# Chaining block products in pairs in PSUM, prelu on ScalarE and VectorE one step apart, and the next splits issued ahead of PSUM copies

## The chip, the cores and the metric

One core of one Trainium2 chip runs the whole program. The metric is the device time of one execution in microseconds (us); the median of three runs before the change is 1681.34 us (1676.72 to 1686.11).

## What is computed

Three stages follow one another. An attention with 32 packed queries per head feeds a first mixture block (product, rational function, product), and its result feeds a second block. The change touches the second block and the passage into it:

```
def _moe2_ref(x, w_in, w_out, alpha):        # x 4608 x 512, w_in 512 x 2048, w_out 2048 x 512
    h = x @ w_in
    g = np.maximum(h, 0.0) + alpha * np.minimum(h, 0.0)     # prelu
    return (g @ w_out).astype(np.float32)
```

## The kernel before

Every product is made of three passes in the fp32r type (`PASSES`): an operand is split into a rounded part (a copy on ScalarE) and the remainder (a subtraction on VectorE or GpSimd). The two parts are needed before a matmul can read the operand.

The second block works on five superblocks of tokens (`SUPER`, index s from 0): four with 2 x 512 tokens and a last one with 2 x 256. A superblock has two halves. The first half (y = 0, called L3 in the code, matmuls in L1018) makes h, the second half (y = 1, L4, matmuls in L1029) makes the output. Each half uses a seven-product block scheme (Strassen and Winograd): products i = 0 to 6, each cut into four pieces n = 0 to 3. A piece is a *unit* of 12 matmuls; a half has 28 units, whose place from 0 to 27 is called the *position* here. `UNITS` holds the order.

In the first half each unit fills a PSUM tile `p` of two banks (pool `psn`, four tiles in turn). When a unit is done, `end_L3` takes it out: a copy or a relu on ScalarE, or an add on VectorE onto a block `v` of h (`add`, L855). Products 0 and 1 share a tile already: the first is copied out, then the second is accumulated onto it in the same banks. Blocks that are complete go through the prelu: `prelu_dve` (two relus on ScalarE, two fused multiply-adds on VectorE, L873) or, for the pieces of products 4 and 3, `prelu_pool` (relu, two scaled copies and relu on ScalarE, L865, L879, L880, then an add on GpSimd, L881). `split_v` splits a block of h for the second half (L947 on ScalarE, L948 on VectorE); `split_y` does it for the input (L781, L782).

All engines execute in program order. The loop over units sets that order: at step u it issues the matmuls of unit u, then `after()` (the taking out of unit u-1), then the tasks that `at(u, ...)` has put there (splits and sums), and in the first superblock `w_split(u + 5)`, which splits a weight tile (L750 ScalarE, L751 GpSimd in the first half and VectorE in the second) that `w_load` had brought. Later superblocks read the split weights back from DRAM by `w_load(u + 12)`.

Before that, the loop over g ends the first mixture block. In its last three rounds (g >= NG, d = 0, 1, 2) it loads and splits the first eight weight tiles through three staging tiles (`s2_tile`).

## Time and profile before

| | |
|---|---|
| profiled execution | 1680.22 us (span of its core 1678.3 us) |
| median of three runs | 1681.34 us |
| second block, first to last matmul | 867.86 to 1674.45 us of the span |
| granted TensorE clock, mean | 0.968 |

Times within the profile are microseconds from the start of the span. PE is TensorE's matmuls, PEld its weight loads, DVE VectorE, ACT ScalarE, POOL GpSimd. The granted clock is a share of full speed. In a timeline, equal neighbours are merged (x7), and a bracket tells how long the engine was idle before the row and what it had waited for. In a table of stretches a row holds the stretch, its length, the busy time and count of PE, PEld, DVE, ACT and POOL, the granted clock, the busy share of the DMA engines and the GB/s that they moved.

### The profile page before, as it was taken

How to read it: one execution, taken by the hardware profiler on the slowest of the kernel's cores; microseconds unless marked ns; L12 is line 12 of the kernel's file. 1: busy time of each engine (PE TensorE's matmuls, PEld its weight loads, DVE VectorE, ACT ScalarE, POOL GpSimd, SP SyncE). 2: the span in 40 equal slices, each digit the busy share in tenths (PEclk: the TensorE clock that was granted, in tenths of full speed). 3: DMA queues.
4: the chain of work that ended last, by engine and by line, in shares of the span. 5: the costliest groups of instructions: out<-in, count | busy, mean ns of one | idle time of the engine just before them, and what ended most of it. 6: DMA issues, size and time to landing. Idle time of an engine off the chain costs nothing.

```text
span 1678.3 us, 20312 instructions
## 1 busy us (share of the span) xinstructions
PE 1534.8 (91%) x7360; PEld 1237.5 (74%) x7360; DVE 1326.0 (79%) x1424; ACT 1036.5 (62%) x1209; POOL 658.0 (39%) x386
## 2 busy tenths in 40 slices
PE   5789869999999999999989779996999799979988
PEld 3444447888888888888868657885888588857878
DVE  5979699899999999999976479665856485648657
ACT  2335377878888888877855765446443744364353
POOL 1113165778788887866665600022001200130020
PEclk9999989999999999999999979998999899989999
DMA  9688822133333333321348447974475447444784
GB/s 346 229 286 280 285 90 76 57 113 120 112 103 114 109 129 99 128 75 51 113 156 294 171 165 273 400 309 148 163 272 182 173 176 253 157 181 158 274 319 139
DMA packets 134404, 305.44 MB, mean 182 GB/s; under 512 B 11680, under 2 KB 63904, under 8 KB 133280
## 3 DMA queue, kind: packets, MB, share of 16 engines
q1 hardware_dynamic: 130848, 291.56, 49.9%
q10 hardware_dynamic: 3456, 12.58, 2.0%
q8 instruction: 59, 0.97, 0.2%
q14 instruction: 41, 0.34, 0.1%
HBM read 221.79 MB, written 82.31 MB: 181 GB/s over the span
## 4 chain that ended last, share of the span: by engine, by line
PE 53%; DVE 23%; ACT 13%; issue 6%; DMA 3%; POOL 1%; SPq 0%; ACTq 0%; DVEq 0%; POOLq 0%
PE p L1029 15%; PE acc L622 13%; PE p L1018 12%; PE h L548 9%; ACT r L865 3%; DVE v L855 3%; DVE vsp L948 2%; ACT r L879 2%; ACT v L880 2%; DVE h L606 2%; DVE s L670 2%; PE pp L329 1%; DVE s L662 1%; ACT vsp L947 1%; DVE s L663 1%
## 5 line engine op out<-in xcount | busy, mean ns | idle before, releaser
L1029 PE MATMUL p<-vsp,ws 128*128 128x512 f32 (+1 forms) x1680 | 379.8, 387 | 59.3 <-issue 25.1
L622 PE MATMUL acc<-gt,wo 128*128 128x512 f32 x1728 | 406.9, 391 | 3.6 <-ACT yo L564 3.6
L1029 PEld LDWEIGHTS p<-vsp,ws 128*128 128x128 f32 x1680 | 307.7, 199 | 131.4 <-issue 31.0
L622 PEld LDWEIGHTS acc<-gt,wo 128*128 128x128 f32 x1728 | 322.1, 188 | 70.3 <-ACT yo L564 4.6
L1018 PE MATMUL p<-ysp,ws 128*128 128x512 f32 (+1 forms) x1680 | 351.5, 371 | 16.6 <-DVE v L855 6.8
L1018 PEld LDWEIGHTS p<-ysp,ws 128*128 128x128 f32 x1680 | 294.6, 190 | 73.0 <-ACT v L887 7.2
L881 POOL TENSOR_TENSOR v<-v,r 128x1024 f32<-128x1024 f32 (+1 forms) x40 | 87.0, 2175 | 610.5 <-ACT v L880 606.5
L548 PE MATMUL h<-a2t,wb 128*128 128x128 f32 (+7 forms) x1536 | 250.7, 319 | 20.1 <-DVE v__1751 L607 5.4
L548 PEld LDWEIGHTS h<-a2t,wb 128*128 128x128 f32 x1536 | 229.3, 192 | 42.5 <-issue 20.0
L948 DVE TENSOR_TENSOR vsp<-v,vsp 128x1024 fp32r<-128x1024 f32 (+1 forms) x140 | 160.5, 1156 | 75.6 <-ACT vsp L947 75.3
L947 ACT ACTIVATE vsp<-v 128x1024 fp32r<-128x1024 f32 (+1 forms) x140 | 132.5, 966 | 108.9 <-PE p L1029 55.3
L855 DVE TENSOR_TENSOR v<-v,p 128x1024 f32<-128x1024 f32 (+1 forms) x120 | 129.8, 1108 | 42.8 <-PE p L1018 42.6
L865 ACT ACTIVATE r<-v 128x1024 f32<-128x1024 f32 (+1 forms) x60 | 58.0, 966 | 162.5 <-DVE v L855 162.5
L873 DVE SCALAR_TENSOR_TENSOR v<-r,nalpha,v 128x512 f32<-128x512 f32 (+1 forms) x80 | 56.4, 747 | 71.6 <-ACT v L870 71.6
L855 DVE TENSOR_TENSOR v<-v 128x1024 f32<-128x1024 f32 (+1 forms) x80 | 88.6, 1113 | 0.0
L502 POOL TENSOR_TENSOR wb<-s,wb 128x512 fp32r<-128x512 f32 x48 | 63.1, 1315 | 31.1 <-ACT wb L501 30.6
L358 POOL TENSOR_TENSOR trn<-trn,mx 128x576 f32<-128x576 f32 x16 | 20.1, 1255 | 111.0 <-DVE mx L357 101.8
L670 DVE SCALAR_TENSOR_TENSOR s<-s,s 128x512 int32<-128x512 int32 x40 | 62.4, 1560 | 0.3
L662 DVE TENSOR_SCALAR s<-s 128x512 f32<-128x512 f32 x40 | 57.5, 1437 | 0.0
L782 DVE TENSOR_TENSOR ysp<-yq,ysp 128x1024 fp32r<-128x1024 f32 (+1 forms) x28 | 37.0, 1325 | 24.6 <-ACT ysp L781 24.6
L409 PE MATMUL pw<-w_in,pph 128*128 128x512 f32 x96 | 50.3, 637 | 4.0 <-ACT wbs L421 3.9
L879 ACT ACTIVATE r<-r,nalpha 128x512 f32<-128x512 f32 (+1 forms) x80 | 50.1, 673 | 1.3
(1032 smaller groups left out, 2353.5 us busy)
## 6 DMA issues: line engine op xcount, KB each, us to landing
ws<-wh_d SPq DMA_DIRECT2D x224, 512.0 KB, 6.1
wh_d<-ws SPq DMA_DIRECT2D x56, 512.0 KB, 4.3
wq_d<-s SPq DMA_DIRECT2D x32, 512.0 KB, 3.8
wb_d<-wbs SPq DMA_DIRECT2D x48, 256.0 KB, 4.9
s<-in_w_out SPq DMA_DIRECT2D x24, 512.0 KB, 4.2
s<-wb_d SPq DMA_DIRECT2D x48, 256.0 KB, 4.0
wst<-wq_d SPq DMA_DIRECT2D x48, 256.0 KB, 3.2
kt<-in_kT SPq DMA_DIRECT2D x16, 576.0 KB, 7.8
```

What stands on the lines that cost most here:

```text
L548: mm(h[:, ft, o:o + m], w[x][:, k, 128 * ft:128 * ft + 128], a2_t[c][:, y, k, o:o + m], start=n == 0, stop=n == 5)
L622: mm(acc[d // 2][:, d % 2, :], w[:, x, 128 * d:128 * d + 128], t[:, y, ft, :], start=f == 0 and (x, y, ft) == (0, 0, 0), stop=f == NP - 1 ...
L662: dve.tensor_scalar(w, w, LOW, HIGH, op0=ALU.max, op1=ALU.min)
L670: dve.scalar_tensor_tensor(wi, in0=words[:, :, 0], scalar=29, in1=wi, op0=ALU.logical_shift_right, op1=ALU.bitwise_or)
L855: dve.tensor_tensor(o, a, b, op=op)
L865: act(r, src, AF.Relu, scale=-1.0)
L879: act(r[:, g], r[:, g], AF.Copy, scale=nalpha[:, f:f + 1])
L881: pool.tensor_tensor(v_, v_, r, op=ALU.add)
L947: act(t[:, 0, :, 0:m], src, AF.Copy)
L948: dve.tensor_tensor(t[:, 1, :, 0:m], src, t[:, 0, :, 0:m], op=ALU.subtract)
L1018: mm(ps[:, g, 0:m], w[:, g, x, 128 * k:128 * k + 128], ysp[s, i](z, k), start=i != 1 and q == 0, stop=q == 5, skip_group_check=i < 2)
L1029: mm(ps[:, d, 0:m], w[:, g, x, 128 * d:128 * d + 128], t[:, z, g, 0:m], start=i != 1 and n == 0 and g == 0 and q == 0, stop=n == 3 and g = ...
```

## The change

1. Two more pairs of products share a PSUM tile in the first half: 3 is accumulated onto 6, and 2 onto 4, in the interleaved order that 0 and 1 had (`ONTO`, `PAIRED`). The blocks of h take the sums as they stand in PSUM, so `end_L3` has one add where product 4 had two, and a sign of the input sums changes.
2. Every prelu is now two relus on ScalarE and two fused multiply-adds on VectorE. `prelu` issues the relus and returns the rest, which the loop issues one step later (`defer`). GpSimd adds and scaled copies are gone.
3. At step u the loop first issues the ScalarE copies of splits (`early`), then `after()`, then the rest of the unit before (`last()`), then sums (`late`), then the subtractions of the splits (`rests`).
4. The splits of the first four units of the second half move from positions 24 to 27 of the first half to 14, 19, 21 and 26. The input's splits and loads move forward, too.
5. The first eight weight tiles are loaded from round d = -1 on, each into a place of its own, and their remainders are made on VectorE. The negation of alpha moves to the same place.

```diff
-    FIRST = ((0, 0), (0, 1), (1, 0), (0, 2), (1, 1), (0, 3), (1, 2), (1, 3))
-    UNITS = [[*FIRST, *((i, n) for i in (5, 6, 4, 3, 2) for n in range(4))],
+    PAIRED = [(x, n) for x, n in ((0, 0), (0, 1), (1, 0), (0, 2), (1, 1), (0, 3), (1, 2), (1, 3))]
+    UNITS = [[((0, 1)[x], n) for x, n in PAIRED] + [(5, n) for n in range(4)] + [((6, 3)[x], n) for x, n in PAIRED]
+             + [((4, 2)[x], n) for x, n in PAIRED],
              [(i, n) for i in (0, 2, 1, 5, 4, 6, 3) for n in range(4)]]
+    ONTO = ({1: 0, 3: 6, 2: 4}, {1: 0})
...
         act(t[:, :, 0], st, AF.Copy)
-        eng.tensor_tensor(t[:, :, 1], st, t[:, :, 0], op=ALU.subtract)
+        return lambda: eng.tensor_tensor(t[:, :, 1], st, t[:, :, 0], op=ALU.subtract)
...
-        if g >= NG:
-            d = g - NG
+        d = g - NG
+        if d == -1:
+            pool.tensor_scalar(nalpha, alpha_sb, -1.0, None, op0=ALU.mult)
+            for n, st in enumerate((gp.tile([128, 2, CH], F32, tag="ast", name="wst", bufs=1),
+                                    spa.tile([128, 2, CH], F32, tag="q_", name="wst", bufs=2))):
+                for x in range(2):
+                    w_load(2 * n + x, st[:, x])
+        elif d >= 0:
             if d == 0:
-                for u in range(3):
-                    w_load(u)
-            else:
-                split_y(0, d - 1, y_block(0, d - 1, 0))
-            for u in range(3 * d, min(3 * d + 3, SOON)):
-                w_split(u, pool)
-                if u + 3 < SOON:
-                    w_load(u + 3)
+                for n, tag in ((2, "v_"), (3, "q_")):
+                    st = spa.tile([128, 2, CH], F32, tag=tag, name="wst", bufs=2)
+                    for x in range(2):
+                        w_load(2 * n + x, st[:, x])
+            for u in range(4 * d, min(4 * d + 4, SOON)):
+                w_split(u, dve)()
+            if d:
+                split_y(0, d - 1, y_block(0, d - 1, 0))()
...
-    def prelu_dve(v_, src, a, n, m):
-        r = neg_part(src, m)
-        act(v_, src, AF.Relu)
...
-    def prelu_pool(v_, a, n, m):
-        r = neg_part(v_, m)
-        for g in range(2):
-            f = HF * a + 2 * n + g
-            act(r[:, g], r[:, g], AF.Copy, scale=nalpha[:, f:f + 1])
-        act(v_, v_, AF.Relu)
-        pool.tensor_tensor(v_, v_, r, op=ALU.add)
+    def prelu(v_, src, a, n, m):
+
+        r = cols(half_tile("r", "r", 3), m)
+        act(r, src, AF.Relu, scale=-1.0)
         act(v_, src, AF.Relu)
...
+        def rest():
+            for g in range(2):
+                f = HF * a + 2 * n + g
+                dve.scalar_tensor_tensor(v_[:, g], in0=r[:, g], scalar=nalpha[:, f:f + 1], in1=v_[:, g], op0=ALU.mult, op1=ALU.add)
+        return rest
...
         elif i == 6:
-            add(v_tile(1, 0, n, m), v12, p)
+            add(v_tile(1, 1, n, m), u2, p)
+        elif i == 3:
+            add(v_tile(1, 0, n, m), u2, p)
+            return prelu(V[1, 0, n], V[1, 0, n], 1, n, m)
         elif i == 4:
-            add(v_tile(1, 1, n, m), V[1, 0, n], p)
-            add(v12, v12, p)
-            prelu_pool(V[1, 1, n], 1, n, m)
-        elif i == 3:
-            add(V[1, 0, n], V[1, 0, n], p, ALU.subtract)
-            prelu_pool(V[1, 0, n], 1, n, m)
+            add(V[1, 1, n], V[1, 1, n], p)
+            return prelu(V[1, 1, n], V[1, 1, n], 1, n, m)
         else:
-            add(v12, v12, p)
-            prelu_dve(v12, v12, 0, n, m)
+            add(u2, u2, p)
+            return prelu(u2, u2, 0, n, m)
...
-        for d, step in ((0, 0), (1, 1), (2, 2), (3, 3), (6, 10), (9, 8), (14, 7), (18, 6)):
-            at(u0 + d, y_sums, s, step)
+        for d in range(4):
+            then(u0 + (0, 0, 1, 3)[d], y_sum, s, d)
+        for d, i in ((3, 5), (6, 6), (7, 3), (9, 4), (10, 2)):
+            at(u0 + d, y_part, s, i)
         if s + 1 < len(SUPER):
-            at(u0 + 20, load_y, s + 1)
+            then(u0 + 13, load_y, s + 1)
         u1 = u0 + NU2
         for d in range(NU2):
-            at(u1 + d - 4, split_v, u1 + d)
+            at(u1 + (d - 4 if d >= 4 else (-14, -9, -7, -2)[d]), split_v, u1 + d)
...
-        if after:
-            after()
+        rests = [f(*args) for f, args in early.pop(u, ())]
+        if u < len(units) and s == 0 and SOON <= u + 5 < 2 * NU2:
+            rests.append(w_split(u + 5, dve if units[u + 5][1] else pool))
+        last, defer = defer, after and after()
+        if last:
+            last()
+        for f, args in late.pop(u, ()):
+            f(*args)
+        for f in rests:
+            f()
+        after = None
```

On PE, in the first half of the first superblock, positions 12 to 19: a row is one unit, p_... its PSUM tile. Before:

```order
L1018 MATMUL p_7456<-ysp_7335,ws_7362 128x512 x12
L1018 MATMUL p_7476<-ysp_7335,ws_7387 128x512 x12
L1018 MATMUL p_7497<-ysp_7335,ws_7410 128x512 x12
L1018 MATMUL p_7521<-ysp_7335,ws_7430 128x512 x12
L1018 MATMUL p_7542<-ysp_7407,ws_7450 128x512 x12
L1018 MATMUL p_7563<-ysp_7407,ws_7470 128x512 x12
L1018 MATMUL p_7591<-ysp_7407,ws_7491 128x512 x12
L1018 MATMUL p_7622<-ysp_7407,ws_7515 128x512 x12
```

and with the change:

```order
L1025 MATMUL p_7458<-ysp_7327,ws_7354 128x512 x12
L1025 MATMUL p_7478<-ysp_7327,ws_7378 128x512 x12
L1025 MATMUL p_7458<-ysp_7352,ws_7405 128x512 x12
L1025 MATMUL p_7525<-ysp_7327,ws_7430 128x512 x12
L1025 MATMUL p_7478<-ysp_7352,ws_7451 128x512 x12
L1025 MATMUL p_7571<-ysp_7327,ws_7471 128x512 x12
L1025 MATMUL p_7525<-ysp_7352,ws_7491 128x512 x12
L1025 MATMUL p_7571<-ysp_7352,ws_7516 128x512 x12
```

Eight tiles filled once each have become four filled twice, with one or two other units between the two fillings.

On VectorE, end of the first half of the second superblock (v<-v,p is the add out of PSUM, the fused rows the prelu, vsp the remainder of a split). Before, steps 14 to 26:

```order
L782 TENSOR_TENSOR ysp<-yq,ysp 128x1024
L855 TENSOR_TENSOR v<-v,p 128x1024 x6
L782 TENSOR_TENSOR ysp<-yq,ysp 128x1024
L855 TENSOR_TENSOR v<-v,p 128x1024 x8
L948 TENSOR_TENSOR vsp<-v,vsp 128x1024
L855 TENSOR_TENSOR v<-v,p 128x1024
L873 SCALAR_TENSOR_TENSOR v<-r,nalpha,v 128x512 x2
L948 TENSOR_TENSOR vsp<-v,vsp 128x1024
```

and with the change, step 21 to the start of step 26:

```order
L868 TENSOR_TENSOR v<-v,p 128x1024
L885 SCALAR_TENSOR_TENSOR v<-r,nalpha,v 128x512 x2
L954 TENSOR_TENSOR vsp<-v,vsp 128x1024
L868 TENSOR_TENSOR v<-v,p 128x1024
L885 SCALAR_TENSOR_TENSOR v<-r,nalpha,v 128x512 x2
L868 TENSOR_TENSOR v<-v,p 128x1024
L885 SCALAR_TENSOR_TENSOR v<-r,nalpha,v 128x512 x2
L868 TENSOR_TENSOR v<-v,p 128x1024
L885 SCALAR_TENSOR_TENSOR v<-r,nalpha,v 128x512 x2
L868 TENSOR_TENSOR v<-v,p 128x1024
L885 SCALAR_TENSOR_TENSOR v<-r,nalpha,v 128x512 x2
L868 TENSOR_TENSOR v<-v,p 128x1024
```

Fourteen adds stood around an input split, and only then came the first split for the second half and the last adds with their prelus; now every add is followed by the prelu of the unit before it, and splits for the second half stand among them.

On ScalarE at the same end (vsp is the rounded part of a split). Before:

```order
L879 ACTIVATE r<-r,nalpha 128x512 x2
L880 ACTIVATE v<-v 128x1024
L865 ACTIVATE r<-v 128x1024
L879 ACTIVATE r<-r,nalpha 128x512 x2
L880 ACTIVATE v<-v 128x1024
L947 ACTIVATE vsp<-v 128x1024
L865 ACTIVATE r<-v 128x1024
L870 ACTIVATE v<-v 128x1024
L947 ACTIVATE vsp<-v 128x1024
L865 ACTIVATE r<-v 128x1024
```

and with the change:

```order
L880 ACTIVATE v<-v 128x1024
L879 ACTIVATE r<-v 128x1024
L880 ACTIVATE v<-v 128x1024
L953 ACTIVATE vsp<-v 128x1024
L879 ACTIVATE r<-v 128x1024
L880 ACTIVATE v<-v 128x1024
L879 ACTIVATE r<-v 128x1024
L880 ACTIVATE v<-v 128x1024
L953 ACTIVATE vsp<-v 128x1024
L879 ACTIVATE r<-v 128x1024
L880 ACTIVATE v<-v 128x1024
L953 ACTIVATE vsp<-v 128x1024 x4
```

The first split for the second half stood behind all eight prelus of products 4 and 3; now the fourth and the fifth split stand among the last prelus, three more stand further ahead, and the later ones follow without a prelu between.

## Rows read from the trace of the kernel before

**Rows 1.** The page, busy time (us), share of the span and instructions of each engine.

```profile
PE 1534.8 (91%) x7360; PEld 1237.5 (74%) x7360; DVE 1326.0 (79%) x1424; ACT 1036.5 (62%) x1209; POOL 658.0 (39%) x386
```

**Rows 2.** Ten half superblocks: us, PE PEld DVE ACT POOL busy (x), clock, DMA, GB/s.

```profile
867.86:967.79 99.93, 81.06 (x338) 64.98 (x336) 57.12 (x44) 60.93 (x81) 59.24 (x35) 0.92 0.68 237
967.79:1062.93 95.14, 86.73 (x337) 67.46 (x337) 81.92 (x87) 53.81 (x66) 0.00 (x0) 0.92 0.70 247
1062.93:1146.52 83.59, 76.60 (x338) 62.83 (x336) 45.91 (x40) 43.67 (x51) 19.18 (x8) 0.98 0.84 332
1146.52:1234.52 88.00, 81.54 (x337) 65.06 (x338) 66.71 (x61) 40.51 (x40) 0.00 (x0) 0.96 0.48 168
1234.52:1318.11 83.59, 76.58 (x338) 62.83 (x336) 45.91 (x40) 43.69 (x51) 19.17 (x8) 0.98 0.63 227
1318.11:1406.12 88.01, 82.52 (x337) 65.95 (x338) 66.71 (x61) 40.52 (x40) 0.00 (x0) 0.95 0.47 167
1406.12:1489.70 83.58, 76.58 (x337) 62.82 (x336) 45.91 (x40) 43.67 (x51) 19.19 (x8) 0.99 0.61 214
1489.70:1578.91 89.21, 83.30 (x337) 66.54 (x337) 65.64 (x61) 39.88 (x40) 0.00 (x0) 0.93 0.46 165
1578.91:1625.60 46.69, 40.70 (x338) 40.35 (x336) 25.90 (x40) 25.70 (x51) 10.30 (x8) 0.99 0.93 361
1625.60:1674.45 48.85, 45.06 (x336) 43.26 (x336) 35.01 (x59) 22.21 (x38) 0.00 (x0) 0.94 0.43 146
```

**Rows 3.** Timeline of PE alone: start, us, instructions merged, idle before and releaser.

```profile
1062.93 60.00 PE L1018 MATMUL p<-ysp,ws 128*128 128x512 f32 x264
1123.26 16.60 PE L1018 MATMUL p<-ysp,ws 128*128 128x512 f32 x72 [0.33 <-PE p L1018]
...
1318.11 8.58 PE L1029 MATMUL p<-vsp,ws 128*128 128x512 f32 x24 [6.67 <-issue]
...
1578.91 31.83 PE L1018 MATMUL p<-ysp,ws 128*128 128x256 f32 x264
...
1655.60 18.85 PE L1029 MATMUL p<-vsp,ws 128*128 128x256 f32 x155 [0.34 <-DVE vsp L948]
```

**Rows 4.** Timeline of all engines, third superblock, end of first half, start of second.

```profile
1289.90 2.59 DVE L782 TENSOR_TENSOR ysp<-yq,ysp 128x1024 fp32r<-128x1024 f32 x1 [3.87 <-ACT ysp L781]
1292.41 7.99 DVE L855 TENSOR_TENSOR v<-v,p 128x1024 f32<-128x1024 f32 x7
...
1300.38 2.41 POOL L881 TENSOR_TENSOR v<-v,r 128x1024 f32<-128x1024 f32 x1 [0.85 <-ACT v L880]
1300.60 1.22 DVE L855 TENSOR_TENSOR v<-v,p 128x1024 f32<-128x1024 f32 x1 [0.19 <-PE p L1018]
...
1313.28 1.04 ACT L947 ACTIVATE vsp<-v 128x1024 fp32r<-128x1024 f32 x1
1313.45 2.34 POOL L881 TENSOR_TENSOR v<-v,r 128x1024 f32<-128x1024 f32 x1 [0.89 <-ACT v L880]
1314.35 2.52 DVE L948 TENSOR_TENSOR vsp<-v,vsp 128x1024 fp32r<-128x1024 f32 x1 [12.53 <-ACT vsp L947]
1316.80 1.21 DVE L855 TENSOR_TENSOR v<-v,p 128x1024 f32<-128x1024 f32 x1
...
1320.28 1.42 DVE L873 SCALAR_TENSOR_TENSOR v<-r,nalpha,v 128x512 f32<-128x512 f32 x2 [2.27 <-ACT v L870]
1321.61 1.22 DVE L948 TENSOR_TENSOR vsp<-v,vsp 128x1024 fp32r<-128x1024 f32 x1
```

**Rows 5.** Timeline of all engines at the start of the first superblock.

```profile
872.00 1.99 ACT L750 ACTIVATE ws<-s 128x512 fp32r<-128x512 f32 x3 [7.60 <-DMA s<-wq_d]
...
880.21 6.10 PE L1018 MATMUL p<-ysp,ws 128*128 128x512 f32 x18 [6.75 <-ACT v L887]
```

**Rows 6.** Timeline of all engines, second half of the first superblock.

```profile
1007.49 0.69 DVE L751 TENSOR_TENSOR ws<-wst,ws 128x512 fp32r<-128x512 f32 x1
```

More of the change, by code (lines that the diff above doesn't have):

```diff
@@ L1018, in attention_then_two_moes @@
                             mm(ps[:, g, 0:m], w[:, g, x, 128 * k:128 * k + 128], ysp[s, i](z, k),
[L1019 removed]
+                               start=not onto and q == 0, stop=q == 5, skip_group_check=again)
                             q += 1
             else:
[L1022 to L1024 removed]
                 t = vsp.pop(u)
@@ L1036, in attention_then_two_moes @@
                 after = lambda a=(s, i, n, ps): end_L3(*a)
-            else:
-                after = (lambda a=(s, i, ps): end_L4(*a)) if n == 3 else None
-            for f, args in tasks.pop(u, ()):
-                f(*args)
-            if s == 0 and u + 5 < 2 * NU2 and u + 5 >= SOON:
-                w_split(u + 5, dve if units[u + 5][1] else pool)
-    assert not tasks
+            elif n == 3:
+                after = lambda a=(s, i, ps): end_L4(*a)
+    assert not early and not late and not defer
     for name in ("spb", "spy", "psn"):
```

100 lines of the change are left out of this document (47 added, 53 removed).

## Prediction

> **What bounds the kernel now.** I read the page's busy times first [rows 1]. PE is busy for 91% of the span and DVE for 79%: PE is the engine to follow, and the question is where its other 9% and its slow stretches lie. Outside the second block the change moves only the last rounds ahead of it, so I cut that block at the starts of its ten halves [rows 2]. The reader is to see there that a first half of a full superblock takes 83.6 us (99.9 in the first superblock) and a second half 88.0 to 95.1, although both issue 336 matmuls of one shape, and that the granted clock is 0.92 to 0.99 in them.
>
> What would a half take without a stop? PE's own timeline [rows 3] shows 264 matmuls in 60.00 us, with no idle time inside: 0.2273 us each, so 336 x 0.2273 = 76.4 us a half and 12 x 0.2273 = 2.73 us a unit. For the last superblock it shows 264 in 31.83 (0.1206 each, 40.5 us) and 155 in 18.85 (0.1216, 40.9 us), 1.45 us a unit. Taken from the lengths in [rows 2]:
>
> - first superblock: 99.93 - 76.4 = 23.5 and 95.14 - 76.4 = 18.7
> - second: 7.2 and 11.6; third: 7.2 and 11.6; fourth: 7.2 and 12.8
> - last: 46.69 - 40.5 = 6.2 and 48.85 - 40.9 = 8.0
>
> Together 114.0 us. This is all that the change can bring, as it takes no matmul away: 1680.2 - 114.0 = 1566.2 us is the floor.
>
> Next, what makes the stops. Around the end of a first half all engines together [rows 4] show one chain. DVE stands 3.87 us for an input split whose rounded part ScalarE had not made, needs 2.59 us for it, and then does seven adds out of PSUM in 7.99 us that had piled up. Behind them ScalarE still has the prelus of products 4 and 3, so the first split for the second half starts on it at 1313.28, its remainder is done at 1316.87, and the next add, which empties the PSUM tile that the second half wants first, ends at 1318.01. PE had stopped 6.67 us before 1318.11 [rows 3]. Then every unit waits for one round of add, relu, relu, fused multiply-adds and split, which shows as DVE's 2.27 us waits. The first 24 matmuls after the stop take 8.58 us where 24 x 0.2273 = 5.46 are needed: they run partly at the lower of the two clock levels (1.2 GHz, against 2.4). In the first superblock ScalarE stands 7.60 us for a weight tile's DMA, the first copy out of PSUM queues behind it, and PE idles 6.75 us [rows 5].
>
> **The change part by part, on DVE.** A row of seven adds in 7.99 us gives 1.14 us for each in a full queue. The two fused multiply-adds and the next instruction start 1321.61 - 1320.28 = 1.33 us apart [rows 4]. I take 1.14 for a split's remainder too.
>
> *Chaining.* Product 4 loses its second add: 4 x 1.14 = 4.6 us of DVE per superblock, which is off the path where DVE keeps up. The new condition: PE may start on a tile again only when the add of the first product has read it. At the tightest places (products 6 and 3, pieces 0 and 3; 4 and 2 likewise) one unit of 2.73 us lies between. The add is first in DVE's step, starts about 0.2 us after the unit's end (idle 0.19 in [rows 4]) and lasts 1.22: 1.4 us, done with 1.3 us to spare, if DVE isn't late by more than that.
>
> *Is DVE late?* From step 20 to 27 each step has one add and one prelu: 1.14 + 1.33 = 2.47 of 2.73 us. The splits at steps 21 and 26 add 1.14 each, so DVE falls 0.9 us behind, regains 0.26 a step, and is 1.1 behind at the end. Steps 28 and 29, with the last prelus, first sums and splits, bring 4.75 and 3.61 us: 3.1, then 4.0 behind, after which a step has 2.28 and it recovers. The split for position 32 is made at step 28: done about 1.1 + 4.75 = 5.9 us after that step's start, where 4 x 2.73 = 10.9 are allowed. The four units before it have splits from steps 14 to 26. So PE should pass from half to half without a stop in the second, third and fourth superblock. In the sum over a half: DVE's 45.9 us [rows 2] plus 12 prelus at 1.33 and three splits at 1.14 make 65.3 of 76.4 us.
>
> *Prelu off GpSimd.* 40 adds on POOL and 80 scaled copies on ScalarE go; ScalarE then has two relus and a split at most in a step. What POOL does besides: the split at 1314.35 takes 2.52 us while POOL runs, the one at 1321.61 takes 1.22 alone, and the add out of PSUM at 1300.60 takes 1.22 in the midst of a POOL add [rows 4]. An instruction of DVE with both inputs in SBUF pays 1.30 us beside POOL. That ends in the later superblocks. In the first one `w_split` stays on POOL up to step 22, and prelus now stand on DVE there. Steps 12 to 22 hold 11 adds, 5 prelus and 3 splits: 22.6 us of 30.0. If all eight instruction groups from SBUF met POOL, 8 x 1.30 = 10.4 us would come on top, 3.0 too many; if half did, nothing. I take 1.5, between 0 and 3.0.
>
> The Trainium skill speaks on this in "SBUF — State Buffer", Who interferes with whom: an instruction of VectorE with two SBUF inputs and one of GpSimd that reads SBUF exclude each other for the whole instruction. The two splits agree with it; by that rule alone, with every group meeting POOL, the term would be the 3.0 and the sum 1583.2.
>
> *First superblock, border and second half.* From step 23 a weight remainder comes to each DVE step (0.69 us [rows 6], 0.6 in a full queue): 3.07 us a step against 2.73, so DVE is 1.7 us behind at step 26 where one unit separates the fillings of the last tile, a stop of 0.3 to 2.6 us. I take 2.0. In the second half sums, splits and remainders make 2.9 us a step for eleven steps; behind by 7 to 8 us, it uses up the 10.9 allowed near position 39. I take 1.0, from 0 to 4.
>
> *Entry.* All eight weight tiles get places of their own and are loaded before the last rounds, so the 7.60 us wait goes. New: their remainders are eight instructions on DVE beside POOL's last work, 8 x 0.6 = 4.8 us, ahead of the input's split. Between 0 and 5 us late; I take 2.5.
>
> *Later superblocks.* The three borders: 0 to 6 each (the old stop is 6.67), I take 1.0 by the step count above, together 3.0. The last superblock has units of 1.45 us; with half the elements an add and a prelu cost somewhat over half, about the unit itself: 0 to 4, I take 1.5. Its weight loads are covered: with PE never waiting in its first half DMA moved 361 GB/s at a share of 0.93 [rows 2]. Small waits like the 0.33 us in [rows 3]: 0.4 a half, 4.0.
>
> **Sum.** What stays: 2.5 + 1.5 + 2.0 + 1.0 + 3.0 + 1.5 + 4.0 = 15.5 us. Gain 114.0 - 15.5 = 98.5, time 1680.2 - 98.5 = 1581.7, say **1582 us**. The profiled execution lies 1.1 us under the median of 1681.34, too little to correct for. All low ends give 1570.5 with the small waits, 1566.5 without; all high ends (5, 3.0, 2.6, 4, 18, 4, 4.0: 40.6) give 1606.8.
>
> **Rivals.**
>
> *DVE becomes the bound.* If a step costs single durations (1.22 + 1.42 = 2.64) and one hand-over like the 0.19 us idle, it is 2.83 of 2.73 us at steps 20 to 27, and with the splits DVE never regains: about 8 x 0.1, two splits at 1.2 and 2.9 for steps 28 and 29, 6 us of stop a border, 30 us over five, and some 10 more in the first superblock's second half, where DVE is busy 81.92 of 95.14 already. 1582 + 40 = 1622, between 1607 and 1640. For: 65 of 76 us is full. Against: seven adds in 7.99 us show no gap where work is queued.
>
> *The chained tiles stop PE (slower).* 40 units (8 a superblock) newly wait for a tile to be read before they may start. If DVE's queue blocks as at 1289.90, 3.87 + 2.59 = 6.46 us before the add, each waits 6.46 - 2.73 = 3.7 us: 40 x 3.7 = 148 us, and 1582 + 148 = 1730. It decides from (1688.6 - 1581.7) / 40 = 2.7 us a unit on: there the time is 8.4 us over before. For: all forty adds stand in one queue with prelus that wait for ScalarE. Against: the prelu comes a step later, when its relus are done, and products 0 and 1 are chained already and show 264 matmuls without a stop [rows 3].
>
> The Trainium skill has a rule for that side in "TensorE: Matmul & The Clock Gate", A second HAM failure mode: psum-queue depth-cycling: a kernel that cycles through PSUM banks idles PE briefly between groups, and its clock goes up and down. The trace doesn't agree yet: the first halves cycle through four tiles, with stops only at the borders.
>
> *It doesn't do what it says.* The stops shift to another place, say splits that wait for their buffers (five for input and blocks together), and most of the 114 us stay: within 8 us of before.
>
> **How the numbers follow.** Forecast (1566 to 1607) 0.74; DVE bound 0.16; stops shifted 0.04; slower 0.06. A measurement of this kernel tells about 0.5%, 8.4 us, from no change. Faster 0.74 + 0.16 = 0.90, same 0.04, slower 0.06. The range goes from 1567, just over the floor, to 1616, which takes in the forecast's high ends and the nearer part of the DVE case: 0.74 + 0.06 = 0.80.
>
> **What would show it.** Right: halves of 76 to 79 us in the second to fourth superblock, a clock of 0.99 or 1.00 in all ten, no PE idle time over 1 us at the change of halves, DVE busy near 65 us in a first half, POOL at 0 after the first superblock. Wrong: PE waits in L1025 for DVE's add at position 14, 19, 22 or 27 (chained tiles), waits in L1033 for DVE's remainder (DVE bound), or a first superblock over 165 us in all (entry or weights).

## The result, and the profile after

The changed kernel takes 1566.31 us (median of four runs, 1563.95 to 1568.25) against 1682.2 us (median of four, 1676.72 to 1686.11: the three known ahead of the prediction and one more): a ratio of 0.9313, 95% interval 0.9283 to 0.9343. The forecast was 1582 us, 1567 to 1616. The sign and the main mechanism came out as forecast; the gain is larger, 115.9 us against 98.5, and the median lies 0.7 us under the range.

The profiled execution took 1565.32 us (span 1563.4). Its page begins with the busy times that answer to [rows 1]:

```profile
PE 1494.1 (96%) x7360; PEld 1221.8 (78%) x7360; DVE 1350.6 (86%) x1492; ACT 995.5 (64%) x1129; POOL 560.8 (36%) x338
```

Cut at the starts of the ten halves, as [rows 2] (columns: us; PE, PEld, DVE, ACT, POOL busy with instructions; clock; DMA share; GB/s):

```profile
862.57:945.28 82.71, 78.61 (x337) 63.79 (x336) 71.59 (x71) 54.47 (x67) 31.67 (x20) 0.98 0.81 285
945.28:1021.70 76.42, 76.42 (x337) 63.24 (x336) 72.87 (x78) 45.73 (x56) 0.00 (x0) 1.00 0.83 297
1021.70:1097.86 76.16, 76.16 (x337) 63.06 (x336) 56.85 (x60) 41.81 (x42) 0.00 (x0) 1.00 0.89 346
1097.86:1174.02 76.16, 76.16 (x338) 63.06 (x336) 59.47 (x54) 33.82 (x33) 0.00 (x0) 1.00 0.59 201
1174.02:1250.18 76.16, 76.16 (x338) 63.06 (x336) 56.85 (x60) 41.81 (x42) 0.00 (x0) 1.00 0.70 240
1250.18:1326.34 76.16, 76.16 (x338) 63.06 (x336) 59.47 (x54) 33.81 (x33) 0.00 (x0) 1.00 0.59 202
1326.34:1402.50 76.16, 76.16 (x338) 63.06 (x336) 56.85 (x60) 41.81 (x42) 0.00 (x0) 1.00 0.68 227
1402.50:1478.66 76.16, 76.16 (x338) 63.06 (x336) 58.41 (x54) 32.95 (x33) 0.00 (x0) 1.00 0.59 202
1478.66:1519.07 40.41, 40.41 (x338) 40.37 (x337) 31.98 (x59) 23.84 (x41) 0.00 (x0) 1.00 0.96 375
1519.07:1559.55 40.48, 40.47 (x338) 40.27 (x336) 31.86 (x53) 18.72 (x31) 0.00 (x0) 1.00 0.60 218
```

From 945.28 us to the end PE's busy time equals the length of every half to 0.01 us: no stop is left, at a clock of 1.00 where [rows 2] had 0.92 to 0.99. The second block takes 696.98 us, 109.6 fewer than the 806.59 of before, and it starts 5.3 us earlier (862.57 against 867.86).

What is left stands in the first superblock. PE's timeline there (start, us, merged instructions, idle before and its releaser):

```profile
862.57 0.61 PE L1025 MATMUL p<-ysp,ws 128*128 128x512 f32 x2
864.60 60.03 PE L1025 MATMUL p<-ysp,ws 128*128 128x512 f32 x262 [1.41 <-DVE ysp L788]
924.83 13.88 PE L1025 MATMUL p<-ysp,ws 128*128 128x512 f32 x60 [0.20 <-DVE v L868]
941.10 4.38 PE L1025 MATMUL p<-ysp,ws 128*128 128x512 f32 x12 [2.38 <-ACT vsp L953]
```

The 2.38 us stop is unit 27's. The profile names a split of ScalarE, whose record ends at 941.02 us; VectorE's own timeline shows the add that frees the tile, unit 25's, from 939.74 to 940.95. The run without the chain (below) decides between the two: there unit 27 has a tile of its own and ends at 945.00, without a stop, before the same split of ScalarE starts at 946.95. So unit 27 waited for the add:

```profile
936.68 1.21 DVE L868 TENSOR_TENSOR v<-v,p 128x1024 f32<-128x1024 f32 x1
...
939.14 0.68 DVE L753 TENSOR_TENSOR ws<-wst,ws 128x512 fp32r<-128x512 f32 x1
939.74 1.21 DVE L868 TENSOR_TENSOR v<-v,p 128x1024 f32<-128x1024 f32 x1
```

Add to add is 3.06 us: the step of 3.07 that the prediction counted with a weight remainder in it.

VectorE at the border of the second superblock, without those remainders:

```profile
1079.02 1.22 DVE L868 TENSOR_TENSOR v<-v,p 128x1024 f32<-128x1024 f32 x1 [0.17 <-PE p L1025]
1080.16 1.41 DVE L885 SCALAR_TENSOR_TENSOR v<-r,nalpha,v 128x512 f32<-128x512 f32 x2
1081.48 1.22 DVE L954 TENSOR_TENSOR vsp<-v,vsp 128x1024 fp32r<-128x1024 f32 x1
1082.62 1.22 DVE L868 TENSOR_TENSOR v<-v,p 128x1024 f32<-128x1024 f32 x1
...
1085.08 1.21 DVE L868 TENSOR_TENSOR v<-v,p 128x1024 f32<-128x1024 f32 x1
...
1087.53 1.21 DVE L868 TENSOR_TENSOR v<-v,p 128x1024 f32<-128x1024 f32 x1
...
1089.99 1.22 DVE L868 TENSOR_TENSOR v<-v,p 128x1024 f32<-128x1024 f32 x1
```

The add at 1079.02 starts 0.17 us after its unit's end, 1078.85. With 2.72 us a unit the next ends are 1081.57, 1084.29, 1087.01, 1089.73, and the adds start 1.05, 0.79, 0.52 and 0.26 us behind them: one split puts VectorE 0.9 us back, each step of 2.46 us regains 0.26. Both numbers stand in the prediction. By step 26, whose add is the one that unit 27 waits for, VectorE has caught up: that add starts at 1092.62, 0.2 us after its unit's end.

### The profile page after: what moved, and what is told of

It reads as the page before. It is cut to its first block, busy times and chain, and to the rows that moved or that the text cites. A ratio compares the mean times of both kernels' runs of the same rounds, so it can differ in the third digit from the quotient of the medians.

```text
span 1563.4 us, 20124 instructions
## 1 busy us (share of the span) xinstructions
PE 1494.1 (96%) x7360; PEld 1221.8 (78%) x7360; DVE 1350.6 (86%) x1492; ACT 995.5 (64%) x1129; POOL 560.8 (36%) x338
## 4 chain that ended last, share of the span: by engine, by line
PE 69%; DVE 20%; issue 4%; ACT 4%; DMA 3%; POOL 0%; SPq 0%; ACTq 0%; DVEq 0%; POOLq 0%
PE p L1033 22%; PE p L1025 20%; PE acc L621 14%; PE h L547 9%; DVE h L605 2%; DVE s L669 2%; DVE s L661 1%; PE pp L328 1%; DVE s L662 1%; PE pw L408 1%; DMA vt<-in_v 1%; DMA kt<-in_kT 1%; DVE s L670 1%; DVE v L885 1%; DVE v L868 1%
## 5 line engine op out<-in xcount | busy, mean ns | idle before, releaser
L1033 PE MATMUL p<-vsp,ws 128*128 128x512 f32 (+1 forms) x1680 | 346.0, 368 | 0.0
L1033 PEld LDWEIGHTS p<-vsp,ws 128*128 128x128 f32 x1680 | 293.0, 189 | 52.6
L953 ACT ACTIVATE vsp<-v 128x1024 fp32r<-128x1024 f32 (+1 forms) x140 | 135.8, 972 | 149.6 <-PE p L1033 102.0
L954 DVE TENSOR_TENSOR vsp<-v,vsp 128x1024 fp32r<-128x1024 f32 (+1 forms) x140 | 156.0, 1114 | 32.3 <-ACT vsp L953 31.8
L868 DVE TENSOR_TENSOR v<-v,p 128x1024 f32<-128x1024 f32 (+1 forms) x100 | 110.8, 1110 | 40.6 <-PE p L1025 40.0
L885 DVE SCALAR_TENSOR_TENSOR v<-r,nalpha,v 128x512 f32<-128x512 f32 (+1 forms) x160 | 112.4, 743 | 29.8 <-ACT v L880 29.8
L880 ACT ACTIVATE v<-v 128x1024 f32<-128x1024 f32 (+1 forms) x60 | 58.6, 976 | 1.9
L868 DVE TENSOR_TENSOR c<-c,p 128x1024 f32<-128x1024 f32 (+1 forms) x25 | 27.4, 1112 | 30.5 <-PE p L1033 30.3
L893 ACT ACTIVATE v<-p 128x1024 f32<-128x1024 f32 (+1 forms) x20 | 18.8, 942 | 54.4 <-PE p L1025 54.4
```

The lines of the kernel that those rows point to most:

```text
L868: dve.tensor_tensor(o, a, b, op=op)
L885: dve.scalar_tensor_tensor(v_[:, g], in0=r[:, g], scalar=nalpha[:, f:f + 1], in1=v_[:, g], op0=ALU.mult, op1=ALU.add)
L953: act(t[:, 0, :, 0:m], src, AF.Copy)
L954: return lambda: dve.tensor_tensor(t[:, 1, :, 0:m], src, t[:, 0, :, 0:m], op=ALU.subtract)
L1033: mm(ps[:, d, 0:m], w[:, g, x, 128 * d:128 * d + 128], t[:, z, g, 0:m], start=not onto and n == 0 and g == 0 and q == 0, stop=n == 3 and g ...
```

## The experiments

The first block varies from run to run by more than several of the effects, so I compare the length of the second block in each profile, first to last matmul: 697.0 us in the changed kernel, and 696.4 in the first run below, which leaves the block as it is. A difference of under 1 us in it therefore shows nothing. A time without a count is of one run. Each part of the change was undone in a run of its own, but for the earlier loads and splits of the input, which no run undoes alone.

**Is the earlier start due to the change?** Two runs move only the multiplication for `nalpha` on GpSimd.

```diff
 (the changed kernel)
     nalpha = top.tile([128, NF], F32, name="nalpha")
+    pool.tensor_scalar(nalpha, alpha_sb, -1.0, None, op0=ALU.mult)
...
-            pool.tensor_scalar(nalpha, alpha_sb, -1.0, None, op0=ALU.mult)
```

> The changed kernel with the multiplication that makes nalpha back at the top of the program on GpSimd, where it was before; nothing else differs. Theory A: the 5.3 us by which the second block starts earlier in the changed kernel (862.6 against 867.9 us) come from this move, since GpSimd waited 2.28 us there for alpha's transfer and held the scaling of the first tiles. Then the second block starts near 867 to 868 us again and the time is about 1571 us. Theory B: the move is worth at most the 0.7 us by which the first matmul starts earlier, and the rest of the 5.3 us is scatter of the first block from run to run (the runs of before spread over 9 us). Then the time stays at 1564 to 1568 us and the second block starts anywhere from 860 to 868 us. The second block itself stays at 697 us by both.

Measured: 1567.72 us (four runs), second block from 864.47. The reverse in the kernel before, `nalpha` in the last round:

> The kernel before with only the making of nalpha moved to the last round of the first block, as the changed kernel has it. Theory A (the move is worth 5 us): about 1676 us and a second block that starts near 862 us. Theory B (scatter): 1677 to 1686 us, second block starting anywhere from 860 to 868 us. By both the second block stays near 807 us long.

Measured: 1678.6 us in ten runs (1674.66 to 1686.89) beside 1678.77 in thirteen of before; ratio 0.9995, interval 0.9973 to 1.0016; second block from 868.97. For this move theory B holds. Over all 18 profiles the second block starts between 861.81 and 868.97 us, and the next pair shows that scatter alone makes a difference of this size. Up to the last rounds of the first block the kernel before with the later `nalpha` and the changed kernel with the old entry (next run) issue the same instructions, yet start 5.7 us apart:

```profile
868.97 5.60 PE L1019 MATMUL p<-ysp,ws 128*128 128x512 f32 x24
```

```profile
863.28 5.60 PE L1021 MATMUL p<-ysp,ws 128*128 128x512 f32 x24
```

A small systematic part isn't excluded: the mean start is 864.1 us over the twelve profiles with the new loading of the weights and 866.0 over the six with the old one (standard deviations 1.4 and 2.8).

**The entry.**

```diff
-            for u in range(4 * d, min(4 * d + 4, SOON)):
-                w_split(u, dve)()
...
+            for u in range(3 * d, min(3 * d + 3, SOON)):
+                w_split(u, pool)()
+                if u + 3 < SOON:
+                    w_load(u + 3, s2_tile())
```

> The changed kernel with the first eight weight tiles loaded as before: three staging tiles, reloaded in turn, remainders on GpSimd, the input's split issued ahead of each group of them. My theory: the entry's stop of 6.75 us comes back (it was 1.41 us with the change), and what follows it in the first superblock shifts with it: 5 to 8 us slower, 1571 to 1574 us. Rival: the first superblock has room for it (the first products need no tile twice), so that the stop is made up by nothing and the border is no better: the same 5 to 8 us. A second rival: the wait was for a late transfer that the other new order removes as well, then within 1 us of 1566.

Measured: 1571.3 us; second block 702.3, 5.3 longer. The stop is back, 6.20 us for ScalarE, which stands 6.09 us for a weight's DMA as in [rows 5]:

```profile
875.08 56.21 PE L1021 MATMUL p<-ysp,ws 128*128 128x512 f32 x240 [6.20 <-ACT v L889]
```

**The deferral by one step.**

```diff
-        last, defer = defer, after and after()
+        last = after and after()
```

> The changed kernel with the fused multiply-adds of the prelu issued in the same step as the add and the relus, not one step later. My theory: where each step has an add and a prelu (products 6, 3, 4 and 2, 16 units of a first half, prelus in 12 of them), VectorE stands from the add's end until ScalarE has made both relus (the 2.27 us waits in the kernel before), so that a step is 1.14 + 2.27 + 1.33 = 4.7 us where there is a prelu and 1.14 where not; from position 20 to 28 eight steps of 4.7 against 2.73 us, chained tiles passing the delay on to PE: 8 x 2.0 = 16 us in each of four full superblocks, 10 in the last, less the slack of some 5 us each: 50 to 75 us slower, 1616 to 1641 us. Rival A: the deferred step hides only what is hidden anyway, as VectorE has 20 us of slack in a first half (56.7 busy of 76.2): within 5 us of 1566. Rival B: two relus queue behind a split's copy in the same step, then up to 6 us a step: over 1660 us.

Measured: 1662.84 us; second block 792.8, 95.8 longer. This undoes most of the gain. VectorE's timeline:

```profile
1111.13 1.21 DVE L868 TENSOR_TENSOR v<-v,p 128x1024 f32<-128x1024 f32 x1
1114.56 1.41 DVE L885 SCALAR_TENSOR_TENSOR v<-r,nalpha,v 128x512 f32<-128x512 f32 x2 [2.22 <-ACT v L880]
1115.89 1.22 DVE L954 TENSOR_TENSOR vsp<-v,vsp 128x1024 fp32r<-128x1024 f32 x1
1117.03 1.21 DVE L868 TENSOR_TENSOR v<-v,p 128x1024 f32<-128x1024 f32 x1
...
1121.79 1.21 DVE L868 TENSOR_TENSOR v<-v,p 128x1024 f32<-128x1024 f32 x1
...
1126.55 1.22 DVE L868 TENSOR_TENSOR v<-v,p 128x1024 f32<-128x1024 f32 x1
```

Add to add is 4.76 us, 5.90 with a split: the 4.7 of my theory, in a time that only rival B reached. The second to the fourth superblock each get 19.2 us longer, where I had 11 (16 less 5 of slack). PE's stops, from position 19 on, are 13.7 to 14.6 us of it, so most of the slack that I took off was not there; the rest is mainly matmuls behind the stops at the lower clock level, such as 12 in 4.58 us at a granted clock of 0.63, which I had left out.

**ScalarE's order.**

```diff
+        last, defer = defer, after and after()
         rests = [f(*args) for f, args in early.pop(u, ())]
...
-        last, defer = defer, after and after()
```

> The changed kernel with each step's work behind the matmuls (ScalarE's copies out of PSUM and relus, VectorE's adds) issued ahead of that step's ScalarE copies for splits, as before the change, and VectorE's parts in the order of the change. My theory: ScalarE is busy 42 of 76 us in a first half, so a split's copy gets at most one add's wait and two relus later, 2 to 3 us, and the splits are needed four units ahead (10.9 us): PE sees it only at the input's splits, 3 to 4 units ahead of their use, and where VectorE's remainder stands in the same step: 0 to 2 us a superblock, 1566 to 1576 us. Rival: this order is what removed the stops at the borders (the 3.87 us wait of VectorE for a rounded part before its seven adds): 15 to 30 us slower, 1581 to 1596 us.

Measured: 1588.62 us; second block 721.1, 24.1 longer: the rival's figure, but 11.4 of it fall in the first superblock, and the stops at a later border are 2.5 us in all, not the 6.67 of before. The order is thus a part of what took those away, not all. In the second superblock ScalarE and VectorE show why:

```profile
1086.55 1.06 ACT L880 ACTIVATE v<-v 128x1024 f32<-128x1024 f32 x1
1087.51 1.04 ACT L953 ACTIVATE vsp<-v 128x1024 fp32r<-128x1024 f32 x1
1088.59 1.22 DVE L954 TENSOR_TENSOR vsp<-v,vsp 128x1024 fp32r<-128x1024 f32 x1 [3.17 <-ACT vsp L953]
1089.73 1.22 DVE L868 TENSOR_TENSOR v<-v,p 128x1024 f32<-128x1024 f32 x1
```

The rounded part stands behind two relus, VectorE waits 3.17 us for it, and the adds behind the remainder come late. I had asked only when the split is needed (four units later), not what is queued behind it.

**GpSimd's part.** Products 3 and 4 go through `prelu_pool` again, with scaled copies on ScalarE and the add on GpSimd, as before.

```diff
-            return prelu(V[1, 0, n], V[1, 0, n], 1, n, m)
+            return prelu_pool(V[1, 0, n], 1, n, m)
...
-            return prelu(V[1, 1, n], V[1, 1, n], 1, n, m)
+            return prelu_pool(V[1, 1, n], 1, n, m)
```

> The changed kernel with the prelu of products 3 and 4 made as before: two relus and two scaled copies on ScalarE, then one add on GpSimd, instead of two relus and two fused multiply-adds on VectorE; the order, the chain and the early splits stay. My theory: VectorE loses 8 x 1.33 = 10.6 us in a first half but every instruction of it with both inputs in SBUF that meets a GpSimd add takes up to 1.30 us longer (2.52 against 1.22 us before), and ScalarE has 4 instructions and a split in a step, over 2.73 us, at positions 20 to 27, so the splits ahead of the border come later. 0 to 4 us a border: 1566 to 1585 us. Rival A: moving the prelu off GpSimd is the part that brings most of the gain (GpSimd takes VectorE's input port): over 1600 us. Rival B: it brings nothing and the time is within 1 us of 1566.

Measured: 1582.01 us; second block 712.0, 15.0 longer, 11.6 of it in the first half of the first superblock: PE stops there for 11.3 us at positions 24 to 27 (2.38 in the changed kernel), at a later border of a full superblock for 0.4. Neither rival, and the time is in my range, but I had 0 to 4 us for that border. The trace shows a chain that I had not thought of: between its adds GpSimd ends a weight's remainder at 926.95 us, the load of a further weight is issued only at 926.98, ScalarE stands 6.04 us for a weight's transfer until 929.07, and VectorE 9.11 us for the split queued behind it. The add behind that split is late, and PE's longest stop is 6.02 us.

**The chain.** Products 3 and 2 in tiles of their own (`ONTO = ({1: 0}, {1: 0})`). The edit makes four adds more in a superblock, one for each piece of product 4 (24 out of PSUM in the third superblock against 20), not the eight that the expectation counts.

> The changed kernel with products 3 and 2 not chained onto 6 and 4 in one PSUM tile: each starts a tile of its own, and VectorE makes the sums with one more add for product 3 and one for product 2 (eight adds more in a first half, 8 x 1.14 = 9.1 us), the rest of the order kept. It computes product 3's V block from V(1,1) and product 2's sum from the stored sum. My theory: VectorE was busy 56.7 of 76.2 us in a first half, so 66 of 76 still fits on the average, but positions 20 to 27 hold 1.14 + 1.33 + up to 1.14 = 2.5 to 3.6 us a step against 2.73, so it gets 2 to 4 us late at the border; with four tiles and no chain a unit waits for the add four units back. 0 to 3 us in each superblock: 1566 to 1580 us. Rival: chaining is the part that brings most of the gain, then over 1600 us. Second rival: without chained tiles no unit waits for the add of its neighbour, so that even the 2.4 us stop of the first border goes: 1563 to 1566 us.

Measured: 1573.84 us; second block 701.5, 4.5 longer. The stop at the first border goes, as the second rival has it, but VectorE's added work makes the second half of that superblock stop for 4.3 us in all, of which:

```profile
959.95 21.59 PE L1034 MATMUL p<-vsp,ws 128*128 128x512 f32 x84 [3.02 <-DVE vsp L955]
```

**The early splits.**

```diff
-            at(u1 + (d - 4 if d >= 4 else (-14, -9, -7, -2)[d]), split_v, u1 + d)
+            at(u1 + d - 4, split_v, u1 + d)
```

> The changed kernel with the first four splits of the second half issued four units ahead, at positions 24 to 27 (as before the change), and not at 14, 19, 21 and 26. My theory: these splits, two instructions each on ScalarE and VectorE, now fall into the steps that hold an add and a prelu: 2.47 + 1.14 = 3.6 us of VectorE in a step against 2.73 us for a unit, four steps running, so VectorE is 3.5 us late at the border, where the first product's split allows about 10.9 us. Then PE stops 0 to 3 us at the border by the chained tiles (one unit of 2.73 us less 1.4 us of add leaves 1.3 us): 0 to 2 us in each of five superblocks, 1566 to 1577 us. Rival: issuing splits early is what took the 6.67 us stops away; then 20 to 30 us slower, 1586 to 1600 us.

Measured: 1571.55 us; second block 701.7, 4.7 longer: 4.03 us at the first border (2.38 before), 0.34 at each of the next three, 0.46 in the last superblock. The time is in my theory's range and far from the rival's; the stop at the first border is above its 3 us.

**VectorE's room.** One more instruction in each step from position 12 on, then two.

```diff
+        if u < len(units) and s > 0 and y == 0 and u % (2 * NU2) >= 12:
...
+            dve.tensor_tensor(junk['x'], junk['x'], junk['x'], op=ALU.add)
```

> The changed kernel with one more VectorE instruction in each step from position 12 to 27 of a first half, in the second to the last superblock: an add of a 128x512 tile that nothing else uses onto itself, some 0.6 us in a full queue (0.6 for a weight remainder of that size). It measures how much room VectorE has at the border. My theory (the step count of the prediction): positions 20 to 27 go from 2.47 to 3.07 us a step against 2.73 for a unit, so VectorE is 8 x 0.34 = 2.7 us and two splits of 1.14 us later, 5.0 us at the border, of which the chained tiles leave 1.3 us: PE stops 1 to 4 us in each of three borders and 2 to 5 us in the last superblock: 1571 to 1583 us. Rival A: VectorE was busy only 56.7 of 76.2 us in a first half, and the time counts on the average: 10 us more are hidden, within 1 us of 1566. Rival B: VectorE is just at the edge and the chained tiles pass all of it on: 16 x 0.6 x 4 = 38 us, near 1604 us.

Measured: 1584.85 us; second block 713.3, 16.3 longer. PE's stops are as in my theory, 2.25 us at each of three borders and 4.36 in the last superblock; the time is 1.9 us over its range, as the matmuls behind some of the stops ran slower (last section).

> As the run with one added VectorE instruction a step, but with two (1.2 us a step). My theory: positions 20 to 27 take 3.67 us a step against 2.73, and 12 to 19 some 3.0: VectorE is 8 x 0.94 + 8 x 0.27 + 2.28 = 12 us late at the border, less 1.3 us: PE stops about 10 us in each of three borders and 10 to 14 us in the last superblock, where the units are 1.45 us and the extra stays 1.2: 1605 to 1612 us. Rival A (the average counts): 56.7 + 19.2 = 75.9 us of 76.2, still hidden in the full superblocks, 10 us in the last: near 1576 us. Rival B (all of it is passed on): 77 us more, near 1643 us.

Measured: 1617.53 us; second block 747.3, 50.3 longer: 11.1 to 11.4 in the second to the fourth superblock, 17.1 in the last, 5.5 us over my range in all. Both are near the step count, if above it, and well off both rivals. With one added instruction PE stops in the same place at three borders for the same 2.25 us (its timeline):

```profile
1100.82 3.04 PE L1025 MATMUL p<-ysp,ws 128*128 128x512 f32 x12 [2.25 <-DVE v L868]
...
1255.71 4.61 PE L1025 MATMUL p<-ysp,ws 128*128 128x512 f32 x12 [2.25 <-DVE v L868]
...
1412.19 4.62 PE L1025 MATMUL p<-ysp,ws 128*128 128x512 f32 x12 [2.25 <-DVE v L868]
```

**Parts alone, in the kernel before.** First all prelus deferred, none on GpSimd.

```diff
-            prelu_pool(V[1, 1, n], 1, n, m)
+            return prelu_dve(V[1, 1, n], V[1, 1, n], 1, n, m)
...
-        if after:
-            after()
+        last, defer = defer, after and after()
+        if last:
+            last()
```

> The kernel before with one part of the change alone: every prelu by two relus on ScalarE and two fused multiply-adds on VectorE, these one step after the add; GpSimd makes none. The products' order and their tiles, the places of the splits, the order of copies and splits within a step and the entry stay as before. My theory, from the runs in which one part was undone: this is the main part (undoing it gave back 96 us), but splits behind copies (22 us), four more adds of VectorE (7 us) and the entry (5 us) stay, and product 4 now takes 2 x 1.14 + 1.33 = 3.6 us a step: 1600 to 1625 us. Rival: the parts only work together: without the early splits and the interleaved order VectorE gets 4 x 0.9 us late with product 4 and the border's stop of 6.7 us stays: 1640 to 1680 us.

Measured: 1639.96 us; second block 765.6, 41.0 shorter than before, at the rival's edge. The 6.7 us stops are gone, but the borders of the second to the fourth superblock show six short ones each, such as:

```profile
1133.65 2.79 PE L1031 MATMUL p<-vsp,ws 128*128 128x512 f32 x11 [0.75 <-DVE vsp L950]
1137.91 0.50 PE L1031 MATMUL p<-vsp,ws 128*128 128x512 f32 x1 [1.47 <-ACT vsp L949]
```

PE waits for each block's rounded part and again for its remainder. Then splits, remainders with them, ahead of the copies, prelus as before:

> The kernel before with one part of the change alone: in each step the splits and sums are issued ahead of the copies out of PSUM and the prelus. Here both parts of a split go ahead, ScalarE's copy and VectorE's remainder. My theory: PE's wait of 6.67 us at the border comes from adds behind a split's remainder that waits for ScalarE (3.87 us), and this goes only in part, since VectorE's adds now stand behind the remainders (1.14 us each) and each step's prelu still waits for its relus: 10 to 40 us faster, 1640 to 1672 us. Rival A: it is worth the 22 us that undoing it cost in the changed kernel: 1655 to 1665 us. Rival B: with the prelus in their own step, VectorE is the slow one anyway, and remainders ahead of adds make PE wait longer for its tiles: slower, over 1690 us.

Measured: 1694.32 us; second block 823.8, 17.2 longer. VectorE's next add waits behind a remainder that waits for ScalarE's prelus:

```profile
1136.72 2.52 DVE L948 TENSOR_TENSOR vsp<-v,vsp 128x1024 fp32r<-128x1024 f32 x1 [11.71 <-ACT vsp L947]
1139.16 1.21 DVE L855 TENSOR_TENSOR v<-v,p 128x1024 f32<-128x1024 f32 x1
```

So rival B, with its time too. Then both parts, with only ScalarE's copies ahead and the remainders last:

> The kernel before with two parts of the change together: all prelus on ScalarE and VectorE with the fused multiply-adds one step later, and in each step ScalarE's copies for splits ahead of the copies out of PSUM, VectorE's remainders last. Products, tiles, places of the splits and entry stay as before. My theory: with the deferral alone (1640 us) what is left at each border is PE waiting for blocks' splits, 0.8 us for a remainder and 1.5 us for a rounded part that stands on ScalarE behind two relus, 8 us in all; the copies ahead take most of that: 3 to 6 us in each of five borders and more in the first second half, 1600 to 1625 us. Rival A: VectorE, with product 4's 3.6 us steps, is what makes the splits late, and the order on ScalarE changes nothing: 1630 to 1640 us. Rival B: as with splits ahead of copies alone (15 to 20 us slower), it makes things worse: over 1650 us.

Measured: 1586.26 us; second block 718.0, 88.6 shorter, better than any theory had it. A later border now loses under 1 us (0.24 and 0.58); the entry (6.40) and the first superblock's second half hold most of the rest.

**Can the rest be had?** The input's split ahead of the weights' remainders at the entry; with it, in the first superblock, two early splits at positions 26 and 27; and the second half's remainders one unit later on top.

> The changed kernel with the input's split ahead of the weights' remainders in the last rounds of the first block. My theory: PE's stop of 1.41 us behind its first two matmuls there is the input's remainder standing behind the weights' remainders on VectorE; it goes, and the second block is 1 to 2 us shorter than 697.0 us. Rival: the input's rounded part on ScalarE is late itself, or the first weights' remainders then are: 696.5 to 699 us.

> As the run with the two splits later, and in the first superblock the second half's weight remainders on VectorE four units ahead, not five, so that none stands in step 23. My theory: 0.6 us less of VectorE ahead of unit 25's add, on top of the 1.14: the stop at position 27 goes from 2.38 to about 0.6 us, second block 693.5 to 696 us, time 1561 to 1566 us as the first block falls (it starts the second block anywhere from 861.8 to 869.0 us so far). Rival: the weight comes too late for the first units of the second half, or VectorE's added lag there stops PE: second block over 698 us.

Measured: second block 695.4 and 695.7 us (697.0 and 696.4 in the two profiles of the changed kernel's block). At the entry 0.90 us stay, now for VectorE's copy of the last `yo`; the border's stop is 2.42 in the first run and 1.15 in the second, but 0.62 come back in the second half. The timed one: 1564.93 us, five runs from 1564.61 to 1567.56, ratio 0.9317 (0.929 to 0.9344): not told apart from the changed kernel's 1566.31. With the two splits moved and the remainders left, the stop was 1.76 and the block 696.0, where the forecast was 694 to 696.5. The input's split is worth about 1 us, at the edge of what this comparison can tell; the two further moves show no gain beyond that.

## Why the prediction missed

Against the profiled execution of before, the gain is 114.9 us: 109.6 in the second block and 5.3 ahead of it. The forecast had 98.5, all in the block. The missing 16.4 us come from three steps.

*The allowances, 8.7 us.* "2.5 + 1.5 + 2.0 + 1.0 + 3.0 + 1.5 + 4.0 = 15.5 us" was to stay; at 76.16 us a half 696.98 - 690.17 = 6.8 us did. In the order of the terms: the entry 1.4; GpSimd in the first superblock 0.2; its border 3.8 (2.38, and 1.46 because the 12 matmuls behind it ran partly at the lower clock level, at a granted clock of 0.65); its second half 0.3; the three later borders, the last superblock and the small waits 0.0; and 1.1 in matmuls of the first half beside the stops. The last three had 8.5 us and measured nothing. They are the step that failed: the step count gave VectorE 1.1 us of lag with 1.3 to spare, thus no stop, and "I take 1.0 by the step count above" put one there all the same. "Small waits like the 0.33 us in [rows 3]" carried a wait of the old order over to the new one. The four terms of the first superblock come to 7.0 us against 6.8 measured there, which is in part luck: its border was 1.8 us too small, since it left out what the matmuls behind a stop lose, and the other three were too large.

*The floor, 2.4 us.* 76.4 us a half came from one stretch of 264 matmuls with its last one's tail in it; without stops a half takes 76.16, and the last superblock 80.9 in place of 81.4.

*The first block, 5.3 us.* It scatters by 7.2 us between profiles, and the profiled run of before was late in it. The range's low end, "just over the floor", took a floor that hangs on one run for a bound. The scatter of the runs shown (9 us) belonged under it. Without these 5.3 us the time would have been inside the range.

What held: the chain of waits at the border (prelus off GpSimd, their deferral and ScalarE's order together bring 88.6 of the 109.6 us), the tiles chained without a wait, the step of 2.47 us (2.46), the lag of 0.9 regained by 0.26, the border of the first superblock as the place that stays, POOL at 0 behind it. One sign of being wrong came as well, in the first superblock alone: the wait for the add at position 27. One reading was wrong without harm: PE was not "never waiting" in the last superblock's first half, it was busy 40.70 of 46.69 us [rows 2]; after the change it is busy throughout, at 375 GB/s. VectorE's load in a later first half did not hold: 65.3 us forecast, 56.9 measured. The groups of its instructions by shape, third superblock, show where (count, busy us and mean ns of one, then idle before). Before:

```profile
L855 DVE TENSOR_TENSOR v<-v,p 128x1024 f32<-128x1024 f32 x21 | 24.9, 1214 | 9.8 <-PE p L1018 9.8
L782 DVE TENSOR_TENSOR ysp<-yq,ysp 128x1024 fp32r<-128x1024 f32 x4 | 6.3, 1563 | 5.2 <-ACT ysp L781 5.2
L873 DVE SCALAR_TENSOR_TENSOR v<-r,nalpha,v 128x512 f32<-128x512 f32 x8 | 5.7, 748 | 7.1 <-ACT v L870 7.1
```

and after:

```profile
L868 DVE TENSOR_TENSOR v<-v,p 128x1024 f32<-128x1024 f32 x19 | 23.1, 1218 | 10.5 <-PE p L1025 10.4
L885 DVE SCALAR_TENSOR_TENSOR v<-r,nalpha,v 128x512 f32<-128x512 f32 x27 | 19.1, 746 | 6.9 <-ACT v L880 6.9
L788 DVE TENSOR_TENSOR ysp<-yq,ysp 128x1024 fp32r<-128x1024 f32 x4 | 4.9, 1220 | 0.3 <-ACT ysp L784 0.3
```

19 fused multiply-adds came, 9.5 prelus and not 12, since the last ones fall into the next half; the adds that the chain takes away were counted under the chain and left out of this sum; and splits beside GpSimd no longer take 1563 ns. By the spacings of the prediction these are some 3.3, 2.3 and, with the first split for the second half (2525 ns before, 1218 after), 2.7 of the 8.4 us.

The rivals: VectorE did not become the bound, but it is near. One more 0.6 us instruction a step costs 16 us, two cost 50. The stop by chained tiles is real but small: the 2.38 us at the first border, which goes without the chain. That a VectorE which blocks in each step stops PE is shown too: without the deferral its prelu waits 2.22 us a step, PE stops behind the adds, and the time is 1662.84 us, under the rival's 1730. How much of that the chain adds is not shown: a step of 4.76 us is longer than a unit of 2.72 with or without it. The rule on cycling through PSUM banks ("A second HAM failure mode: psum-queue depth-cycling" in the Trainium skill's "TensorE: Matmul & The Clock Gate") did not decide here: the four tiles are filled in turn for 614 us at a granted clock of 1.00.

GpSimd's term had its mechanism. In the first superblock a pair of fused multiply-adds that meets a weight remainder on GpSimd takes 2.44 to 2.46 us, alone 1.40; VectorE's and GpSimd's timelines:

```profile
921.10 2.46 DVE L885 SCALAR_TENSOR_TENSOR v<-r,nalpha,v 128x512 f32<-128x512 f32 x2
...
929.24 1.40 DVE L885 SCALAR_TENSOR_TENSOR v<-r,nalpha,v 128x512 f32<-128x512 f32 x2
```

```profile
921.66 1.35 POOL L753 TENSOR_TENSOR ws<-wst,ws 128x512 fp32r<-128x512 f32 x1 [2.76 <-ACT ws L752]
```

Several of these cost VectorE 1.05 us each, and PE 0.20 us once.

The parts are not additive. Undone one by one, prelu deferral, ScalarE's order, GpSimd, entry, early splits and chain give back 95.8, 24.1, 15.0, 5.3, 4.7 and 4.5 us, together 149.4 and not 109.6. My reading is that most of them guard the same slack of VectorE; no run undoes two at once.

## What to carry to other kernels

Where an engine in order needs another's answer within a step, issue what needs it one step later, and put the producer's copy at the head of its queue and the consumer's half at the tail of its own: in this kernel the first, with the prelus moved off GpSimd, gives 41 of 110 us, with the copies at the head and the remainders at the tail 89, and splits put ahead whole, without the first, lose 17. The deferral without the move off GpSimd was not run in the kernel before; undone alone in the changed kernel, the deferral costs 95.8 us and the move 15.0. Count the work of the tight steps, not the average of the stage; VectorE at 57 of 76 us had under 0.6 us a step to spare at the border. When such a count gives no stop, forecast none, and put the doubt, with the scatter of the runs, into the range on both sides.

## What was not expected of the hardware

Equal stops cost unequal time. In the run with one added VectorE instruction, three stops of 2.25 us at the same place were followed by 12 matmuls in 3.04, 4.61 and 4.62 us. The granted clock of those stretches (columns: us, PE busy, clock, DMA share, GB/s):

```profile
1100.80:1103.70 2.90, 2.88 (x13) 1.00 0.14 54
1255.70:1260.10 4.40, 4.39 (x12) 0.61 0.11 43
1412.20:1416.60 4.40, 4.40 (x12) 0.61 0.12 47
```

The clock stayed at the upper level after the first and was partly at the lower (1.2 against 2.4 GHz) after the other two, though PE had been busy without a stop for 152 to 154 us ahead of each. The same holds for the stop at the first border: in the changed kernel 12 matmuls took 4.38 us after 2.38 us of it, with the early `nalpha` 3.00 after 2.42. Why stays open. And the first block, with the same instructions, ends up to 5.7 us apart in two profiles. The earlier one has 1595 matmuls in the first 400 us and the later one 1562; from 400 to 860 us both have the same PE busy time, 454.42 and 454.45 us, so the difference arises in the first 400.
